# One spectral and bilinear block on one core: four edits to who computes what in the column groups

## The chip, the cores and the metric

The kernel runs on one core of a Trainium2 chip. The core has five engines with queues of their own: PE (TensorE, matmuls; PEld is its weight load), DVE (VectorE), ACT (ScalarE), POOL (GpSimd) and SP (SyncE, which here only issues DMAs). The metric is the device time of one execution in microseconds (us); lower is better. Three executions of the kernel before took 687.51, 687.57 and 688.01 us, with a median of 687.57.

## The reference

The input is one sequence x of 2048 rows and 640 columns in float32. Two residual blocks follow each other, each behind a layer normalisation without weights:

```python
h = x + irfft2(rfft2(layernorm(x)) * (w_r + 1j * w_i))
h2 = h + ((layernorm(h) @ w_gate) * (layernorm(h) @ w_up)) @ w_down
```

The first is a filter in the two-dimensional Fourier domain, the second a gated unit with 1728 hidden columns and no nonlinearity.

## The kernel before

The work runs in stages, all written for the sixteen row tiles of 128 rows.

Stage 1 (to about 39 us) loads and normalises x, folds the columns by symmetry and multiplies by a table `crs`. Its results are copied by ACT from PSUM into `s1` (`s1_copy`, L254).

The *column groups* (about 39 to 114 us) are the sixteen steps g = 0 to 15 that the change touches. For each group PE runs three pieces:

- `d_mm(g)`: the row transform, four matmuls with the table `tab` (the main part) and four with `frt` (the remainder part). It writes a PSUM pair `y`. The remainder needs `s1r`, a copy of `s1[:, 4]` split into a rounded high part and what is left, the low part. `part(g, n, engine)` makes it for n groups, for each of two halves of 64 partitions: a cast (L260) and a subtraction (L261) that reads the cast's result. Groups 0 to 2 were done on DVE, the later ones on POOL (called at the even g for groups g+5 and g+6).
- `s2_mm(g)` (L360): two matmuls on `t`, ACT's copy of the row transform (`d_out`, L353). It writes a PSUM tile, `u` or `v` (the two *twins*, one buffer each), or a pair `y` for the last two groups.
- `is2_mm(g)` (L385): the inverse products on the filtered group, into the other twin; into a pair `y` for groups 13 and 15. The first half of the pair gets the main products and the second half the remainder products.

Between the last two, DVE filters the group (`filt`, four operations): `y = v*w` (L368), the two cross products into `us` on 64 partitions each (L369, L370), and the sum `y + us` (L371). The first three read the PSUM tile and end its use; the sum has both operands in SBUF. The result `Y[g]` lies in a ring of four slots in SBUF, so group g overwrites what group g-4 left. Behind `is2_mm`, `is2_out` copies the main products into `qm` (L415, ACT) and splits the remainder products into `qr`: ACT copies them to SBUF (L420), POOL moves one row (L421), casts (L422) and subtracts (L423). For group 15 the main copy is shared by ACT (L415) and DVE (L417), and ACT and DVE split from PSUM (L427 to L431).

The order is written out in a loop over g: `s2_mm(g)`, `d_mm(g+2)`, `is2_mm(g-lag)`, `filt(g)`. `lag` begins at 0 and is raised at g = 0, 5 and 9; these three *lag steps* run no `is2_mm`, and the variable `flip` is set there: the twins change their parts, so that the next `s2_mm` writes the twin that the current filter does not read. In all other steps `s2_mm(g+1)` writes the tile that `filt(g)` reads, and waits for its L370. After the loop groups 11 to 15 are finished (L484 to L495).

Then comes the inverse row transform (to about 160 us): for each row tile `id_main` (reads `qm`, L526), `id_rest` (reads `qr`, L531), an unfolding on DVE and ACT and `is1_mm`. Its PSUM tiles are the twins in turn, with one pair `y` for tile 2. The gated unit fills the rest of the time, almost all of it PE.

Of the kernel before, what the change touches and what calls it, by code (L numbers as in the profile page):

```python
# [13 lines left out]
AF = mybir.ActivationFunctionType  # L14
OP = mybir.AluOpType

P = 128
S, D, NF, FF = 2048, 640, 321, 1728
NT = S // P
NG = 16  # L20
NQ = 322
# [27 lines left out]
def f32(ap):  # L49
    return ap.bitcast(F32)  # L50
# [11 lines left out]
def tile_spectral_glu(ctx: ExitStack, tc: tile.TileContext, x, wf, wgu, wlast, wdown, wdlast,  # L62
                      cc, ci, fmain, frem, imain, irem, mm, out):
    nc = tc.nc
# [6 lines left out]
    tt, act = nc.vector.tensor_tensor, nc.scalar.activation  # L71
# [3 lines left out]
    def banks(key, name, side="left"):  # L75
        if key in pools:
            open_pools[key].close()
        open_pools[key] = ExitStack()
        pools[key] = open_pools[key].enter_context(tc.tile_pool(name=name, bufs=2, space=bass.MemoryType.PSUM, side=side))
# [4 lines left out]
    def pair(tag):  # L84
        return pools["y"].tile([P, 2, 512], F32, tag=tag, name=tag, bufs=2)
# [4 lines left out]
    def wk(shape, name):  # L90
        return work.tile(shape, F32, tag="wk", name=name)
# [22 lines left out]
    def home(tag, shape, name, dt=F32):  # L114
        return keep.tile(shape, dt, tag=tag, name=name)

    def cut(t, o, *shape):
        v = t[:, o:o + int(np.prod(shape))]
        names = [f"d{i}" for i in range(len(shape))]
        return v.rearrange(f"p ({' '.join(names)}) -> p {' '.join(names)}", **dict(zip(names[1:], shape[1:])))  # L120
# [86 lines left out]
    def folded(t):  # L207
        o = t % NR * 1030 + 2
        return fold[:, o:o + 642], fold[:, o + 644:o + 1028]
# [44 lines left out]
            act(view(s1, 4 * t + 2048 * c, [[2048, e - c], [64, 32], [1, 4]]),  # L254
                ps[:, c * P:e * P].rearrange("p (c g m) -> p c g m", c=e - c, g=32), AF.Copy)

    def part(g, n, engine):
        for rows, k in ((slice(0, 64), 0), (slice(64, 128), 1)):
            src, hi, lo = s1[rows, 4, g:g + n], s1r[rows, k, g:g + n], s1r[64 * (1 - k):64 * (2 - k), k, g:g + n]
            engine.tensor_copy(hi, src)  # L260
            engine.tensor_tensor(lo, src, f32(hi), op=OP.subtract)  # L261

    turn = [0]

    def twin(k):
        return pools["a"].tile([P, 2, 512], F32, tag=("u", "v")[k], name=("u", "v")[k], bufs=1)
# [13 lines left out]
    for g, ts in enumerate(GROUPS):  # L280
        n = len(ts)
# [19 lines left out]
        else:  # L301
            o = crs[:, ts[0] * P:(ts[0] + n) * P].rearrange("p (t m) -> p t m", t=n)
            steps[f"t{g}"] = lambda o=o, r=r, n=n: tt(o, view(cct, 0, [[0, n], [1, P]]), view(r, 0, [[1, n], [0, P]]),
                                                      op=OP.mult)
# [6 lines left out]
    for k in order:  # L311
        if k[0] == "h":
            if k[2:] in TINY:
                done = TINY[k[2:]]
            else:
                f, j = folded(int(k[3:]))
# [3 lines left out]
            steps[k]()  # L320
    room.clear()
    banks("y", "ptwo")
    part(0, 1, nc.vector)

    WM, WI = {}, {}

# [12 lines left out]
    PD, T, PU, Y, PI = {}, {}, {}, {}, {}  # L339

    def d_mm(g):
        ps = PD[g] = pair("y")
        for c, (b, i) in enumerate(((1, 1), (1, 0), (0, 1), (0, 0))):
            mmx(ps[:, b, i * NH:(i + 1) * NH], s1[:, c, g], fmt[:, c], i == 1, False)
        for b in (1, 0):
            for l in range(2):
                mmx(ps[:, b, 0:NQ], s1r[:, 1 - b, g], frt[:, l, b], False, l == 1)

    def d_out(g):
        t = T[g] = wk([P, 2, NQ], "t")  # L350
        for c in range(2):
            for h in range(2):
                act(t[64 * c:64 * c + 64, h].rearrange("p (b f) -> p b f", b=2),  # L353
                    PD[g][64 * h:64 * h + 64, :, c * NH:(c + 1) * NH], AF.Copy)
# [6 lines left out]

    ring = [cut(home("spare", [P, 2576], "ring"), 0, 4, 2, NQ)]

    def filt(g):
        v, w = PU[g][:, :, 0:NQ], WM[g][1]
        y = Y[g] = ring[0][:, g % 4]
        us = wk([P, 2, NQ], "us")
        tt(y, v, w[:, 0], op=OP.mult)  # L368
        nc.vector.scalar_tensor_tensor(us[0:64], v[64:128], -1.0, w[64:128, 1], op0=OP.mult, op1=OP.mult)  # L369
        tt(us[64:128], v[0:64], w[0:64, 1], op=OP.mult)  # L370
        tt(y, y, us, op=OP.add)  # L371

    def is2_mm(g, k=0):
        both = pair("y") if g in (NG - 3, NG - 1) else twin(k)
        pm, pr = both[:, 0], both[:, 1]
        PI[g] = pm, pr

        def o(ps, n, c, h):
            return ps[0:n, c * 256:(c + 1) * 256].rearrange("p (a m) -> p a m", m=8)[:, :, 4 * h:4 * h + 4]

        y = Y[g]

        def one(ps, n, c, a):
            for h in range(2):
                nc.tensor.matmul(o(ps, n, c, h), y[:, h, a:a + n], inv(g, h), start=True, stop=True)  # L385

        if g == NG - 1:
            second = PI[NG - 3][0]
            PI[g] = (pm, second), pr
            one(pm, P, 0, 194)  # L390
            one(second, P, 0, 1)
            one(pr, 65, 0, 129)
            return
        one(pr, 65, 0, 129)
        one(pm, P, 0, 194)
        one(pm, P, 1, 1)

    def inv(g, h):
        return WI[g][:, h].rearrange("p (a m) -> p a m", m=4)

    def is2_out(g):
        pm, pr = PI[g]
        f = stage[g % 2]
        hi, lo = (qr[n:n + 64, :, :, 8 * g:8 * g + 8] for n in (0, 64))

        def rest(ap):
            return ap[:, 0:256].rearrange("p (r n m) -> p r n m", r=2, n=NT)

        def main(engine=None, half=None):
            o, i = qm[:, :, :, 8 * g:8 * g + 8], pm  # L410
            if half is not None:
                o, i = o[:, 2 * half:2 * half + 2], pm[half][:, 0:256]
            i = i.rearrange("p (c n m) -> p c n m", c=4 if half is None else 2, n=NT)
            if engine is None:
                act(o, i, AF.Copy)  # L415
            else:
                engine.tensor_copy(o, i)  # L417

        def split():
            act(f[0:65], pr[0:65, 0:256], AF.Copy)  # L420
            nc.gpsimd.tensor_copy(f[32:33, 128:256], f[64:65, 0:128])  # L421
            nc.gpsimd.tensor_copy(hi, rest(f[0:64]))  # L422
            nc.gpsimd.tensor_tensor(lo, rest(f[0:64]), f32(hi), op=OP.subtract)  # L423

        def split_last():
            e = f[32:33, 0:128].rearrange("p (n m) -> p n m", n=NT)
            act(hi, rest(pr[0:64]), AF.Copy)  # L427
            act(f[32:33, 0:128], pr[64:65, 0:128], AF.Copy)
            tt(lo, rest(pr[0:64]), f32(hi), op=OP.subtract)
            nc.vector.tensor_copy(hi[32:33, 1], e)  # L430
            tt(lo[32:33, 1], e, f32(hi[32:33, 1]), op=OP.subtract)  # L431

        return main, split_last if g == NG - 1 else split
# [2 lines left out]
        load_wm(g)  # L436
        load_wi(g)
    d_mm(0)
    part(1, 2, nc.vector)
    part(3, 2, nc.gpsimd)  # L440
    d_out(0)
    d_mm(1)
    d_out(1)
# [1 line left out]
    for g in range(NG - 2):  # L445
        s2_mm(g)
        d_mm(g + 2)
        if g + 3 == NG:
            xt = home("big", [P, 2, 5, 2, 512], "xt", F32R)
            irt = xt[:, 1].rearrange("p k l n -> p (k l n)")[:, 0:5 * NQ].rearrange("p (c q) -> p c q", c=5)  # L450
            nc.gpsimd.dma_start(irt, irem)
            s2_mm(NG - 2)
        if g in (0, 5, 9):
            lag += 1
            back = None
            flip = 1
        else:
            back = g - lag
            flip = 0
            is2_mm(back, 1 - turn[0])  # L460
        filt(g)
        if g % 2 == 0 and g + 5 < NG:
            part(g + 5, min(2, NG - g - 5), nc.gpsimd)
        if g + 3 < NG:
            load_wm(g + 3)
        d_out(g + 2)
        if back is not None and g + 3 < NG:
            main, split = is2_out(back)
            split()
            main()  # L470
            load_wi(back + 3)
        turn[0] ^= flip
        if g == 6:
            nc.sync.dma_start(cit, ci)
            nc.sync.dma_start(imt, imain)
            load_wi(NG - 2)
            load_wi(NG - 1)
    s2_mm(NG - 1)
    main, split = is2_out(NG - 6)
# [4 lines left out]
    for g, k in ((NG - 5, 1 - turn[0]), (NG - 4, turn[0]), (NG - 3, 0), (NG - 2, 1 - turn[0])):  # L484
        is2_mm(g, k)
        if g == NG - 5:
            filt(NG - 1)
        main, split = is2_out(g)
        split()
        main()  # L490
    is2_mm(NG - 1)
    main, split = is2_out(NG - 1)
    main(half=0)
    main(nc.vector, 1)
# [23 lines left out]
    PE_, PY, YT, Z = {}, {}, {}, {}  # L518

    def id_main(t, half=(0, 1)):  # L520
        if 0 in half:
            PE_[t] = pair("y") if t == 2 else twin((t - (t > 2) + turn[0]) % 2)
        ps = PE_[t]
        for c, (b, o) in enumerate(((0, 0), (1, 0), (0, 161), (1, 161))):
            if c // 2 in half:
                mmx(ps[:, b, o:o + 161], qm[:, c, t], imt[:, c], c < 2, False)  # L526
# [6 lines left out]
    def id_mm(t):  # L533
        id_main(t)
        id_rest(t)
# [577 lines left out]
    for n, (blk, p) in enumerate(steps):  # L1113
        if p == 6:
            s13, s12 = 2, 0
            if blk == 0:
# [27 lines left out]
                hi, lo = t34(0)  # L1144
                hi()
            else:
# [36 lines left out]
                hi, lo = t34(0)  # L1183
# [190 lines left out]
```

## Time and profile before

| what | value |
|---|---|
| median of three executions | 687.57 us |
| the profiled execution, time | 687.77 us |
| the profiled execution, span on the core | 686.0 us |
| granted TensorE clock | 0.999 |
| busy share of the span: PE, DVE, ACT, POOL | 98%, 69%, 45%, 55% |

The span runs from the first to the last instruction that the profiler recorded; the execution's own time is 1.8 us longer. All terms of the prediction are made against this one execution.

A row of the timeline reads: start in us, duration in us, engine, line, operation, output and inputs by the program's names, shapes, count, and in brackets how long the engine had been idle before, and what ended that. A row of the windows reads: the stretch in us, its length, then the busy time of PE, PEld, DVE, ACT and POOL in it with their instructions, the granted clock, and the DMA's share and rate. The matmul pieces overlap at their ends: the next one's start lies before the last one's recorded end.

### The profile page before, as it was taken

To read this page: it belongs to the slowest core of one execution; us is meant where nothing else is said; L and a number is where in the kernel's file an instruction comes from. 1 tells how busy PE (TensorE), PEld (TensorE's weight loads), DVE (VectorE), ACT (ScalarE), POOL (GpSimd) and SP (SyncE) were. 2 spreads that over 40 slices of the span, in tenths; PEclk is the share of its full clock that TensorE was granted. 3 is DMA by queue.
4 is the path that set the end of the run, shared out by engine and by line. 5 is a ranking of instruction groups with operands and counts; after the bars stand their busy time and mean duration, and the time that the engine had idled before them with its cause. 6 is when DMAs were issued, how large, how long until landed. Compare 5 with 4: busy or idle time off the path is not lost.

```text
span 686.0 us, 9960 instructions
## 1 busy us (share of the span) xinstructions
PE 674.0 (98%) x3740; PEld 593.8 (87%) x3740; DVE 471.5 (69%) x821; ACT 306.1 (45%) x568; POOL 378.9 (55%) x368
## 2 busy tenths in 40 slices
PE   8999999999999999999999999999999999999998
PEld 8888888887898988888888989888888888888987
DVE  7978887998965657576666658644757666565654
ACT  7956563488633334334334263342343333435220
POOL 2127634000296695959596534088595959778510
PEclk9999999999999999999999999999999999999999
DMA  9517771014111212121210353301212111030203
GB/s 331 199 43 227 255 245 64 1 59 147 44 59 38 78 39 77 39 77 39 77 40 28 108 208 124 130 1 39 77 38 78 39 61 55 2 114 0 77 1 153
DMA packets 23231, 60.26 MB, mean 88 GB/s; under 512 B 2576, under 2 KB 7184, under 8 KB 23184
## 3 DMA queue, kind: packets, MB, share of 16 engines
q1 hardware_dynamic: 22608, 57.92, 24.4%
q0 software_dynamic: 288, 1.48, 0.7%
q8 instruction: 29, 0.48, 0.3%
q10 hardware_dynamic: 288, 0.23, 0.1%
q14 instruction: 18, 0.15, 0.1%
HBM read 51.76 MB, written 7.86 MB: 87 GB/s over the span
## 4 chain that ended last, share of the span: by engine, by line
PE 90%; DVE 5%; DMA 3%; issue 1%; ACT 0%; POOL 0%
PE e L97 49%; PE y L97 30%; PE v L97 2%; PE u L97 2%; DMA x<-in_x_dram 2%; PE v L360 1%; PE u L385 1%; DVE us L370 1%; DVE us L369 1%; DVE ring L368 1%; PE f L229 1%; DMA bits<-in_mm_dram 1%; PE e L592 1%; PE u L360 1%; DMA cct<-in_cc_dram 1%
## 5 line engine op out<-in xcount | busy, mean ns | idle before, releaser
L97 PE MATMUL e<-xt,wst 128*128 128x512 f32 x864 | 220.4, 392 | 0.0
L97 PEld LDWEIGHTS e<-xt,wst 128*128 128x128 f32 x864 | 157.7, 188 | 26.7
L97 PE MATMUL y<-wd,ht 128*128 128x320 f32 x832 | 144.6, 311 | 0.1
L97 PEld LDWEIGHTS y<-wd,ht 128*128 128x128 f32 x832 | 131.0, 188 | 13.3 <-DVE xb L993 1.1
L782 POOL TENSOR_TENSOR wst<-raw,wst 128x1024 fp32r<-128x1024 f32 x24 | 57.8, 2409 | 130.5 <-ACT wst L781 117.7
L97 PE MATMUL e<-t,wst 128*128 128x512 f32 x288 | 75.1, 393 | 0.0
L798 POOL TENSOR_TENSOR wst<-raw,wst 128x896 fp32r<-128x896 f32 (+1 forms) x46 | 65.2, 1441 | 5.1 <-ACT wst L793 5.1
L993 DVE TENSOR_TENSOR x<-y,x 128x640 f32<-128x640 f32 x60 | 48.9, 822 | 25.6 <-PE y L97 25.2
L993 DVE TENSOR_TENSOR xb<-y,xb 128x640 f32<-128x640 f32 x60 | 49.0, 823 | 25.4 <-PE y L97 24.3
L814 ACT ACTIVATE ht<-e 128x512 fp32r<-128x512 f32 x48 | 27.5, 596 | 73.7 <-DVE rawh L911 49.7
L97 PEld LDWEIGHTS e<-t,wst 128*128 128x128 f32 x288 | 52.4, 188 | 8.8
L1081 DVE TENSOR_TENSOR m<-e,m 128x512 f32<-128x512 f32 x24 | 16.5, 687 | 50.6 <-ACT m L1074 33.4
L97 PE MATMUL y<-ex,ht 128*128 128x320 f32 x240 | 48.2, 309 | 0.0
L793 ACT ACTIVATE wst<-raw 128x896 fp32r<-128x896 f32 (+1 forms) x48 | 30.1, 677 | 34.5 <-POOL raw L787 33.7
L818 DVE TENSOR_TENSOR ht<-e,ht 128x512 fp32r<-128x512 f32 x48 | 33.1, 689 | 16.7 <-ACT ht L814 16.2
L949 ACT ACTIVATE wd<-draw 128x640 fp32r<-128x640 f32 x20 | 14.8, 741 | 65.6 <-POOL draw L962 53.9
L97 PEld LDWEIGHTS y<-ex,ht 128*128 128x128 f32 x240 | 40.2, 188 | 3.5
L97 PE MATMUL e<-xt,wdir 128*128 128x512 f32 x180 | 41.9, 391 | 0.2 <-DVE q L547 0.2
L818 POOL TENSOR_TENSOR ht<-rawh,ht 128x512 fp32r<-128x512 f32 x20 | 25.8, 1292 | 26.9 <-ACT ht L814 26.9
L97 PEld LDWEIGHTS e<-xt,wdir 128*128 128x128 f32 x180 | 33.5, 188 | 7.3 <-issue 0.6
L97 PE MATMUL e<-ht,wst 128*128 128x512 f32 x144 | 39.0, 394 | 0.0
L353 ACT ACTIVATE t<-y 64x322 f32<-64x322 f32 x64 | 27.7, 433 | 24.8 <-PE y L97 24.2
(228 smaller groups left out, 1216.4 us busy)
## 6 DMA issues: line engine op xcount, KB each, us to landing
raw<-in_wgu_dram SPq DMA_DIRECT2D x24, 640.0 KB, 3.9
wts<-in_wf_dram SPq DMA_DIRECT2D x16, 644.0 KB, 4.1
draw<-in_wdown_dram SPq DMA_DIRECT2D x24, 320.0 KB, 4.5
x<-in_x_dram SPq DMA_DIRECT2D x16, 320.5 KB, 6.0
bits<-in_mm_dram SPq DMA_DIRECT2D x32, 128.0 KB, 4.3
sp<-x SPq DMA_DIRECT2D x8, 320.0 KB, 2.2
xb<-sp SPq DMA_DIRECT2D x8, 320.0 KB, 5.5
out_dram<-x SPq DMA_DIRECT2D x8, 320.0 KB, 2.2
```

The source lines that it names most:

```text
L97: nc.tensor.matmul(o, l, r, start=start, stop=stop, skip_group_check=True)
L229: nc.tensor.matmul(PS1[t][k > 1 and t == LAST][:, k // 4, k % 4 * P:k % 4 * P + P], l, c, start=n == 0, stop=n == len(ls) - 1)
L353: act(t[64 * c:64 * c + 64, h].rearrange("p (b f) -> p b f", b=2), PD[g][64 * h:64 * h + 64, :, c * NH:(c + 1) * NH], AF.Copy)
L360: nc.tensor.matmul(ps[h][:, 0:NQ], WM[g][0][:, h], T[g][:, h], start=True, stop=True)
L782: nc.gpsimd.tensor_tensor(wa[:, 1], stage[:, 0:1024], f32(wa[:, 0]), op=OP.subtract)
L793: act(ws[:, 0, o:o + b - a], stage[:, a:b], AF.Copy)
L798: ptt(ws[:, 1, o:o + b - a], stage[:, a:b], f32(ws[:, 0, o:o + b - a]), op=OP.subtract)
L814: act(unit(u)[0], src, AF.Copy)
L818: engine.tensor_tensor(lo, src, f32(hi), op=OP.subtract)
L949: act(w[:, 0, a:b], r, AF.Copy)
L993: tt(xv, PQ[q][:, :, 0:320], xv, op=OP.add)
L1081: tt(m5, acc_a, m5, op=OP.add)
```

## The change

Four edits, all in the column groups:

1. `part` gets a fourth argument, the operation that makes the high part. For groups 0 to 2 that is now an ACT copy; the subtractions stay on DVE. For the others both stay on POOL.
2. At the three lag steps the filter's sum (`y + us`) is issued to POOL instead of DVE.
3. Group 14's filter result gets a tile of its own (from the pool `wk`) instead of a ring slot, and its split of the remainder products goes from POOL to DVE.
4. The remainder products of group 15 go to the second half of a twin instead of the second half of the pair that takes the main products. With that, the PSUM tiles of the inverse row transform are renumbered: tile 0 takes the twin `u`, tile 1 the pair `y`, and then `v` and `u` in turn.

The cut diff:

```diff
-    def part(g, n, engine):
+    def part(g, n, engine, copy):
...
-            engine.tensor_copy(hi, src)
+            copy(hi, src)
             engine.tensor_tensor(lo, src, f32(hi), op=OP.subtract)
+
+    def act_copy(o, i):
+        act(o, i, AF.Copy)
...
-    part(0, 1, nc.vector)
+    part(0, 1, nc.vector, act_copy)
...
-    def filt(g):
+    def filt(g, engine=nc.vector):
...
-        y = Y[g] = ring[0][:, g % 4]
+        y = Y[g] = ring[0][:, g % 4] if g != NG - 2 else wk([P, 2, NQ], "y")
...
-        tt(y, y, us, op=OP.add)
+        engine.tensor_tensor(y, y, us, op=OP.add)
...
-            second = PI[NG - 3][0]
+            second, pr = PI[NG - 3][0], twin(k)[:, 1]
...
-        def split():
+        def split(engine=nc.gpsimd):
...
-    part(1, 2, nc.vector)
-    part(3, 2, nc.gpsimd)
+    part(1, 2, nc.vector, act_copy)
+    part(3, 2, nc.gpsimd, nc.gpsimd.tensor_copy)
...
-        filt(g)
+        filt(g, nc.gpsimd if flip else nc.vector)
...
-        split()
+        split(nc.gpsimd if g < NG - 2 else nc.vector)
         main()
-    is2_mm(NG - 1)
+    is2_mm(NG - 1, turn[0])
...
-            PE_[t] = pair("y") if t == 2 else twin((t - (t > 2) + turn[0]) % 2)
+            PE_[t] = pair("y") if t == 1 else twin((t - (t > 1) + turn[0] + 1) % 2)
```

The lines behind `filt` stand three lower in the changed kernel: its L371 to L374 are L368 to L371 of before, L388 is L385, L423 is L420.

Three places show what moved. The first is DVE's queue at the end of stage 1, where the remainder parts of groups 0 to 2 are made, and then the first filter. Before:

```order
L246 TENSOR_TENSOR fold<-fold 128x2x160
L260 CAST s1r<-s_82 64x128
L261 TENSOR_TENSOR s1r<-s_82,s1r 64x128
L260 CAST s1r<-s_82 64x128
L261 TENSOR_TENSOR s1r<-s_82,s1r 64x128
L260 CAST s1r<-s_82 64x256
L261 TENSOR_TENSOR s1r<-s_82,s1r 64x256
L260 CAST s1r<-s_82 64x256
L261 TENSOR_TENSOR s1r<-s_82,s1r 64x256
L368 TENSOR_TENSOR ring<-u,wts 128x644
```

The same place in the changed kernel, down to the second filter:

```order
L246 TENSOR_TENSOR fold<-fold 128x2x160
L261 TENSOR_TENSOR s1r<-s_82,s1r 64x128 x2
L261 TENSOR_TENSOR s1r<-s_82,s1r 64x256 x2
L371 TENSOR_TENSOR ring<-u,wts 128x644
L372 SCALAR_TENSOR_TENSOR us<-u,wts 64x644
L373 TENSOR_TENSOR us<-u,wts 64x644
L371 TENSOR_TENSOR ring<-v,wts 128x644
```

The four casts have left DVE (they stand in ACT's queue between the last copy of stage 1 and the first `d_out`), and the second filter follows the first one's third operation.

The second place is POOL's queue from the parts of groups 3 and 4 to the first split. Before:

```order
L260 CAST s1r<-s_82 64x256
L261 TENSOR_TENSOR s1r<-s_82,s1r 64x256
L260 CAST s1r<-s_82 64x256
L261 TENSOR_TENSOR s1r<-s_82,s1r 64x256
L260 CAST s1r<-s_82 64x256
L261 TENSOR_TENSOR s1r<-s_82,s1r 64x256
L260 CAST s1r<-s_82 64x256
L261 TENSOR_TENSOR s1r<-s_82,s1r 64x256
L421 COPY bits<-bits 1x128
```

And in the changed kernel:

```order
L260 CAST s1r<-s_82 64x256
L261 TENSOR_TENSOR s1r<-s_82,s1r 64x256
L260 CAST s1r<-s_82 64x256
L261 TENSOR_TENSOR s1r<-s_82,s1r 64x256
L374 TENSOR_TENSOR ring<-ring,us 128x644
L260 CAST s1r<-s_82 64x256
L261 TENSOR_TENSOR s1r<-s_82,s1r 64x256
L260 CAST s1r<-s_82 64x256
L261 TENSOR_TENSOR s1r<-s_82,s1r 64x256
L424 COPY bits<-bits 1x128
```

The sum of group 0 stands between the parts of groups 3 and 4 and those of groups 5 and 6, which ran without a break before; the sums of groups 5 and 9 stand likewise ahead of later parts.

The third place is DVE's queue from the last filter's sum to the split of group 15. Before:

```order
L371 TENSOR_TENSOR ring<-ring,us 128x644
L417 COPY qm<-y 128x32x8
L429 TENSOR_TENSOR qr<-y,qr 64x32x8
L430 CAST qr<-bits 1x16x8
L431 TENSOR_TENSOR qr<-bits,qr 1x16x8
```

And in the changed kernel:

```order
L374 TENSOR_TENSOR ring<-ring,us 128x644
L424 COPY bits<-bits 1x128
L425 CAST qr<-bits 64x32x8
L426 TENSOR_TENSOR qr<-bits,qr 64x32x8
L420 COPY qm<-y 128x32x8
L432 TENSOR_TENSOR qr<-v,qr 64x32x8
```

Group 14's split, three operations, now stands on DVE between the last sum and DVE's half of group 15's main copy (L420 in the changed kernel).

More of the change, by code (lines that the diff above doesn't have):

```diff
@@ L417, in main @@
                 engine.tensor_copy(o, i)
-        def split():
+        def split(engine=nc.gpsimd):
             act(f[0:65], pr[0:65, 0:256], AF.Copy)
-            nc.gpsimd.tensor_copy(f[32:33, 128:256], f[64:65, 0:128])
-            nc.gpsimd.tensor_copy(hi, rest(f[0:64]))
-            nc.gpsimd.tensor_tensor(lo, rest(f[0:64]), f32(hi), op=OP.subtract)
+            engine.tensor_copy(f[32:33, 128:256], f[64:65, 0:128])
+            engine.tensor_copy(hi, rest(f[0:64]))
+            engine.tensor_tensor(lo, rest(f[0:64]), f32(hi), op=OP.subtract)
         def split_last():
@@ L460, in tile_spectral_glu @@
             is2_mm(back, 1 - turn[0])
-        filt(g)
+        filt(g, nc.gpsimd if flip else nc.vector)
         if g % 2 == 0 and g + 5 < NG:
-            part(g + 5, min(2, NG - g - 5), nc.gpsimd)
+            part(g + 5, min(2, NG - g - 5), nc.gpsimd, nc.gpsimd.tensor_copy)
         if g + 3 < NG:
```

## Prediction

> **What bounds the kernel now.** I began with the page. The profiled execution took 687.77 us around a span of 686.0; the three timed runs have a median of 687.57.
>
> ```profile
> span 686.0 us, 9960 instructions
> PE 674.0 (98%) x3740; PEld 593.8 (87%) x3740; DVE 471.5 (69%) x821; ACT 306.1 (45%) x568; POOL 378.9 (55%) x368
> ```
>
> PE is busy for 98% of the span, so nothing pays that does not shorten or close a pause of PE. The change touches only the column groups, from 38.7 to about 114 us, so next I asked which waits PE has between 36 and 115 us (columns: total, times, longest).
>
> ```profile
> PE y L97 <- DVE s1r L261: 1.5, 2, 0.8
> PE u L360 <- DVE us L370: 0.8, 1, 0.8
> PE v L360 <- DVE us L370: 0.7, 2, 0.4
> PE y L385 <- DVE ring L371: 0.6, 1, 0.6
> PE v L97 <- ACT qm L415: 0.5, 1, 0.5
> ```
>
> These are 4.1 us in all, and each line answers to one part of the change. The pauses cost more than their idle time, because matmuls overlap when they flow and restart without overlap. So I cut the stage at the starts of PE's pieces, read off the PE timeline, and compared the length of equal pieces. The first two numbers after the stretch are its length and PE's busy time.
>
> ```profile
> 38.75:41.88 3.13, 2.42 (x15) 1.75 (x14) 2.22 (x5) 0.55 (x2) 2.08 (x4) 1.00 0.00 0
> 41.88:44.60 2.72, 1.94 (x14) 1.69 (x13) 2.17 (x4) 1.73 (x4) 2.44 (x5) 1.00 0.00 0
> 45.69:47.37 1.68, 1.68 (x14) 1.68 (x13) 1.47 (x2) 0.86 (x2) 0.00 (x0) 1.00 0.21 57
> 47.37:51.93 4.56, 4.26 (x30) 3.75 (x29) 4.45 (x7) 3.29 (x8) 0.00 (x0) 1.00 0.56 168
> 51.93:56.11 4.18, 4.18 (x28) 3.84 (x29) 3.36 (x5) 2.08 (x6) 3.05 (x7) 1.00 0.71 236
> 56.11:60.21 4.10, 4.10 (x31) 3.77 (x30) 3.30 (x5) 2.66 (x7) 2.54 (x4) 1.00 0.65 227
> 67.09:72.14 5.05, 4.26 (x30) 3.76 (x29) 4.94 (x7) 3.76 (x10) 3.16 (x5) 1.00 0.66 228
> 83.19:87.88 4.69, 4.27 (x31) 3.77 (x29) 4.58 (x7) 3.42 (x8) 2.42 (x5) 1.00 0.71 235
> 105.26:106.59 1.33, 1.33 (x14) 1.33 (x13) 1.30 (x3) 0.86 (x2) 1.19 (x3) 1.00 0.90 347
> 106.59:108.66 2.07, 1.49 (x14) 1.30 (x12) 1.98 (x2) 1.32 (x4) 1.87 (x4) 1.00 0.05 12
> 108.66:110.73 2.07, 1.59 (x12) 1.35 (x12) 0.42 (x1) 0.84 (x3) 1.80 (x5) 1.00 0.00 0
> ```
>
> The row transform of one group (d_mm) takes 1.68 us when nothing stops it; those of groups 0 and 1 take 3.13 and 2.72. A full group takes 4.10; the groups behind the three lag steps take 4.56, 5.05 and 4.69, and the group behind such a pause 4.18, so 0.08 more each. One group's inverse product (is2_mm) takes 1.33; the last two pieces take 2.07 each. What could be won is therefore 1.45 + 1.04 (remainder parts), 0.54 + 1.03 + 0.67 (lag steps), 0.74 + 0.74 (end): 6.2 us.
>
> **Part 1: the high parts on ScalarE.** The handover at the start, engine by engine:
>
> ```profile
> 38.95 0.55 ACT L254 ACTIVATE s<-u 128x256 f32<-128x256 f32 x2 [0.48 <-PE u L229]
> 39.53 0.22 DVE L260 CAST s1r<-s 64x128 fp32r<-64x128 f32 x1 [2.06 <-ACT s L254]
> 39.79 0.37 DVE L261 TENSOR_TENSOR s1r<-s,s1r 64x128 fp32r<-64x128 f32 x1
> 40.09 0.72 POOL L261 TENSOR_TENSOR s1r<-s,s1r 64x256 fp32r<-64x256 f32 x1
> 40.19 0.72 DVE L260 CAST s1r<-s 64x128 fp32r<-64x128 f32 x1
> 41.48 0.56 PE L97 MATMUL y<-frt,s1r 128*128 128x322 f32 x2 [0.71 <-DVE s1r L261]
> 42.14 1.78 ACT L353 ACTIVATE t<-y 64x322 f32<-64x322 f32 x4 [2.63 <-PE y L97]
> 42.27 0.55 DVE L261 TENSOR_TENSOR s1r<-s,s1r 64x256 fp32r<-64x256 f32 x1
> ```
>
> The same cast takes 0.22 us on DVE alone and 0.72 beside GpSimd's subtraction. Now four ACT copies replace the four DVE casts. ACT idled 2.63 us there. The nearest row for an ACT copy of this size (busy us, then mean ns of one):
>
> ```profile
> L427 ACT ACTIVATE qr<-y 64x256 fp32r<-64x256 f32 x1 | 0.4, 365 | 0.0
> ```
>
> At 0.37 us apiece for 256 columns, and less for 128, all four are done by 41.0 (39.5, where ACT's last copy of the stage before ends, and four times 0.37). DVE's first subtraction then runs from about 39.9 to 40.3; the second ends at 40.8 if it follows at once (0.37 to 0.55 by the rows of DVE's L261), or at 41.4 if GpSimd's 0.72 subtraction goes in between. Before, PE got it at 41.48. So the first transform wins between 0.1 and 0.7 us. The third and fourth subtraction, 0.55 each, end by 41.9, or by 43.2 if GpSimd goes in between once more (41.4 + 0.55 + 0.72 + 0.55). The second transform starts 0.1 to 0.7 us before 41.88 and needs the fourth for its last two matmuls, at the earliest 1.68 - 0.56 = 1.12 us on: 42.3 to 42.9. Its 1.04 goes whole, or all but 0.3. d_out(0), the ACT piece at 42.14 behind 2.63 us of idling, can follow PE at once, since ACT is through with its copies by then. Sum 0.85 to 1.75; I take 1.4, somewhat above the middle, because a loss at both transforms needs GpSimd to go first twice.
>
> The Trainium skill ("SBUF — State Buffer", Who interferes with whom) says that a DVE instruction with two SBUF inputs and a GpSimd instruction that reads SBUF exclude each other for a whole instruction; by that rule GpSimd would get in between each time that it started first, and this term would be nearer to 0.85.
>
> **Part 2: three sums on GpSimd.** At a lag step two filters follow each other on DVE with only 2.77 us of PE work between their inputs (4.10 without the 1.33 of is2_mm), and the fourth operation of the first holds up the second. The four operations:
>
> ```profile
> L371 DVE TENSOR_TENSOR ring<-ring,us x16: 828/830/1323, 48.4 to 107.4; 128x644 f32<-128x644 f32 x16
> 47.57 0.82 DVE L370 TENSOR_TENSOR us<-u,wts 64x644 f32<-64x644 f32 x1
> 50.14 1.49 PE L385 MATMUL u<-bits,ring 128*65 128x128 f32 x12
> L953 POOL TENSOR_TENSOR wd<-draw,wd 128x640 fp32r<-128x640 f32 x20 | 31.1, 1576 | 0.0
> ```
>
> Without the sum, 0.83 to 1.32 us, DVE can begin the next filter as soon as its input is there. In a flowing group the chain of input, three operations and release fits: PE has no wait there but those listed. How near it is, the group that starts at 51.93 tells: its first operation starts at 53.29 (a row further down), three operations at 0.83 end 2.5 us later, 3.85 after the group's start, and 4.10 are to be had. So all three pauses should go, by a margin of 0.25 less the release of PE. GpSimd's price for 128x644 I take from the 128x640 row: 1.58. Its sums for groups 5 and 9 are used two to three groups later, over 6 us: hidden. That of group 0 is not: shifted by part 1's gain (1.4) with everything else, L370 ends at 47.0, GpSimd starts 0.1 later and ends at 48.7; is2_mm(0) wants it at 48.7, its weight load 0.15 before. So 0.2 to 0.25 of the 0.54 comes back as a new wait: term 0.3, range 0 to 0.54. The other two: 1.03 and 0.67. Queued behind each sum on GpSimd are remainder parts and splits; they slip behind the sum's end, at group 0 to 48.7 us, but the parts so delayed are for group 5, whose transform PE runs in iteration 3, two to three groups of 4.1 us later. That covers it; without that cover each us of slip would be a us of wait.
>
> **Part 3: the end of the groups.** The rows:
>
> ```profile
> 101.55 0.83 DVE L368 TENSOR_TENSOR ring<-y,wts 128x644 f32<-128x644 f32 x1 [0.72 <-PE u L385]
> 107.38 1.23 DVE L371 TENSOR_TENSOR ring<-ring,us 128x644 f32<-128x644 f32 x1
> 108.20 0.38 ACT L420 ACTIVATE bits<-u 65x256 f32<-65x256 f32 x1 [0.47 <-PE u L385]
> 109.93 0.42 DVE L417 COPY qm<-y 128x256 f32<-128x256 f32 x1 [1.32 <-PE y L385]
> 110.30 0.38 ACT L415 ACTIVATE qm<-y 128x256 f32<-128x256 f32 x1 [1.23 <-PE y L385]
> ```
>
> The filter of group 14 waited 0.72 us for is2_mm(10), whose ring slot it overwrites; with a tile of its own it doesn't. Then the last sum starts at about 106.6 and ends at 107.4 (at 0.83) to 107.9 (at 1.3), all on the clock of before. PE can begin group 15 at 106.59 + 1.33 = 107.92. The 0.74 goes, or 0.5 of it: I take 0.67.
>
> The other 0.74 stands before id_main(0), which waited for ACT's copy at 110.30, and that waited for the remainder products that shared its tile. In the other bank pair they no longer hold it: with PE's start at 107.92 the copy ends near 109.4. But DVE's copy of the other half (L417) now stands behind group 14's split, three new DVE operations that cannot start before ACT's copy at 108.20 has ended (108.58): about 0.22 + 0.22 to 0.72 + 0.37 to 0.55 us, by the DVE casts and subtractions of part 1, that is until 109.4 to 110.1, and later by another 0.72 if GpSimd's subtraction for group 13 gets in between. L417 ends 0.42 later, between 109.8 and 111.2. id_main(0) wants it half way through its piece, about 0.6 after its start (an estimate: half of a piece a little shorter than is2_mm's 1.33), at 107.92 + 1.33 + 0.6 = 109.85. So 0 to 1.3 us of new waiting stands against 0.74: term 0.05, range -0.5 to 0.74.
>
> **Behind the groups.**
>
> ```profile
> 110.70:152.00 41.30, 41.27 (x255) 36.98 (x256) 38.09 (x108) 22.70 (x49) 1.32 (x4) 1.00 0.05 21
> DVE q L546 <- ACT s L542: 2.0, 1, 2.0
> ```
>
> In the next stage PE and DVE (third busy time) are both close to full. DVE's run starts after a 2.0 us wait for ACT, which waits for PE, so it moves along with PE, and the gain is kept to the end.
>
> **Sum.** 1.4 + 0.3 + 1.03 + 0.67 + 0.67 + 0.05 = 4.1 us. 687.77 - 4.1 = 683.65 for a profiled execution, which stood 0.2 above the median: 683.45. With all lower ends (0.85, 0, 0.95, 0.59, 0.5, -0.5; the lag steps without what the next group loses) 2.4 us, 685.2; with all upper ends (1.75, 0.54, 1.03, 0.67, 0.74, 0.74) 5.5 us, 682.1.
>
> **Rivals.** *The end gives its share back and GpSimd gets between all subtractions and comes late with its first sum*: lower ends throughout, 685.2. For it: casts three times as long beside GpSimd. Against: it needs all of them. Chance 0.13.
>
> *DVE keeps the gain.* DVE is nearly as full as PE in the stage behind (38.09 of 41.30 us); if its run starts when it did, nothing arrives: 687.6. Against: the wait at its head, which PE sets. Chance 0.06.
>
> *GpSimd's sum shuts out DVE* (the slower side). If DVE's three filter operations of the next group stand still while a sum of length h runs, each lag step loses h against the flowing case: 687.57 - 2.1 (parts 1 and 3) - 2.24 + 3h. At 1.58 that is 688.0, within 0.2%; it turns slower from h = 1.9; stretched by 0.5 as the cast was (0.72 against 0.22), h is 2.08 and the time 689.5.
>
> ```profile
> 53.29 0.83 DVE L368 TENSOR_TENSOR ring<-v,wts 128x644 f32<-128x644 f32 x1 [0.76 <-PE v L360]
> 53.45 0.73 POOL L423 TENSOR_TENSOR qr<-bits,qr 64x256 fp32r<-64x256 f32 x1
> ```
>
> For it: L371's 1.32 and the 0.72 cast. Against: these two rows, a filter operation with an operand in PSUM at its usual 0.83 beside a GpSimd subtraction at its usual 0.73; only L371, with both operands in SBUF, is ever stretched, and that is the one that leaves. Chance 0.06: 0.05 slower, 0.01 the same.
>
> **How the numbers follow.** The forecast has 0.75, the first rival 0.13; both are faster. About 0.2%, 1.4 us, is what a measurement tells here from no change. Faster 0.88, same 0.07, slower 0.05. The range runs from 682.2 to 685.3, which holds the forecast's ends and the first rival.
>
> **What would show it.** Right: no PE wait for s1r of over 0.4 us; groups behind the lag steps at 4.1 to 4.2; L368-L370 (now L371 to L373) still 0.83 beside the sums; a wait of 0.1 to 0.3 at is2_mm(0); id_main(0) waiting for DVE instead of ACT. Wrong: filter operations stretched beside a GpSimd sum, waits of PE between 111 and 152 us that were not there, or a sum much over 1.6 us.

## The result and the profile after

The changed kernel took 683.68 us (median of four executions, 683.30 to 683.78), the kernel before 687.54 beside it: the ratio is 0.9942, with a 95% interval from 0.9925 to 0.9959. That is 3.86 us faster, where 4.1 were forecast. Times here are medians; of all executions behind them one, of the kernel with the sums alone, was slow (834.03 us at a granted clock of 0.753), and it moves that kernel's median from 685.06 to 685.13. The profiled execution took 683.78 us around this span:

```profile
span 682.0 us, 9958 instructions
PE 673.3 (99%) x3740; PEld 593.9 (87%) x3740; DVE 469.0 (69%) x817; ACT 307.7 (45%) x572; POOL 382.3 (56%) x368
```

The waits of PE in the changed kernel between 30 and 165 us:

```profile
PE u L97 <- DVE qm L420: 0.7, 1, 0.7
PE e L97 <- DVE q L550: 0.2, 1, 0.2
PE y L97 <- DVE s1r L261: 0.2, 1, 0.2
```

Of the five lines of before, four are gone or nearly so: the lag steps (L370, now L373) and the last sum (L371, now L374) appear no more, and s1r is down from 1.5 to 0.2. The fifth has changed its releaser: PE now waits 0.7 us for DVE's copy, not for ACT's. The same cut of PE's pieces as in the prediction, in the changed kernel (stretch, length, PE busy first):

```profile
38.94:41.56 2.62, 2.41 (x15) 1.74 (x14) 1.43 (x3) 2.00 (x6) 1.58 (x4) 1.00 0.00 0
41.56:43.25 1.69, 1.69 (x15) 1.69 (x13) 0.97 (x2) 1.45 (x4) 0.72 (x1) 1.00 0.00 0
46.03:50.22 4.19, 4.19 (x31) 3.72 (x30) 3.85 (x6) 2.94 (x7) 2.86 (x4) 1.00 0.53 153
50.22:54.32 4.10, 4.10 (x30) 3.76 (x29) 3.21 (x5) 2.43 (x7) 3.67 (x7) 1.00 0.81 268
65.31:69.40 4.09, 4.09 (x30) 3.76 (x29) 3.74 (x6) 2.84 (x7) 3.20 (x5) 1.00 0.68 230
69.40:73.53 4.13, 4.13 (x30) 3.79 (x29) 3.31 (x5) 2.53 (x7) 2.95 (x5) 1.00 0.91 281
80.42:84.52 4.10, 4.10 (x31) 3.76 (x29) 3.76 (x6) 2.85 (x7) 3.13 (x6) 1.00 0.70 227
84.52:88.65 4.13, 4.13 (x31) 3.79 (x30) 3.31 (x5) 2.53 (x7) 2.26 (x4) 1.00 0.80 267
103.18:104.51 1.33, 1.33 (x14) 1.33 (x13) 1.05 (x2) 0.86 (x2) 1.24 (x2) 1.00 0.07 20
104.51:106.07 1.56, 1.50 (x14) 1.25 (x12) 0.74 (x2) 1.16 (x4) 1.35 (x4) 1.00 0.00 0
106.07:108.21 2.14, 1.47 (x8) 1.23 (x9) 2.00 (x5) 0.62 (x2) 1.00 (x3) 1.00 0.00 0
```

Three pieces of before are needed beside those that the prediction shows, the groups behind the pauses at groups 5 and 9 and id_main(0):

```profile
72.14:76.32 4.18, 4.18 (x28) 3.85 (x29) 3.36 (x5) 1.62 (x5) 1.65 (x3) 1.00 0.82 252
87.88:92.06 4.18, 4.18 (x28) 3.84 (x29) 3.37 (x5) 1.96 (x6) 1.40 (x3) 1.00 0.67 226
110.73:111.94 1.21, 1.21 (x9) 1.21 (x10) 0.64 (x2) 0.48 (x2) 1.00 (x3) 1.00 0.00 0
```

Set against the same pieces of before, each term of the sum can be read off (in us):

| term | before | after | won | forecast |
|---|---|---|---|---|
| transforms of groups 0 and 1 | 3.13 + 2.72 | 2.62 + 1.69 | 1.54 | 1.4 |
| lag step at group 0 | 4.56 + 4.18 | 4.19 + 4.10 | 0.45 | 0.3 |
| lag step at group 5 | 5.05 + 4.18 | 4.09 + 4.13 | 1.01 | 1.03 |
| lag step at group 9 | 4.69 + 4.18 | 4.10 + 4.13 | 0.64 | 0.67 |
| up to group 15's products | 2.07 | 1.33 | 0.74 | 0.67 |
| those products and id_main(0) | 2.07 + 1.21 | 1.56 + 2.14 | -0.42 | 0.05 |

The sum is 3.96 us. The last line is the one that came out other than taken: the end gives back 0.42 us. The rows of the changed kernel there:

```profile
105.30 0.43 DVE L424 COPY bits<-bits 1x128 f32<-1x128 f32 x1 [1.03 <-ACT bits L423]
105.73 0.72 POOL L426 TENSOR_TENSOR qr<-bits,qr 64x256 fp32r<-64x256 f32 x1
105.76 0.83 DVE L425 CAST qr<-bits 64x256 fp32r<-64x256 f32 x1
106.63 0.42 DVE L426 TENSOR_TENSOR qr<-bits,qr 64x256 fp32r<-64x256 f32 x1
107.08 0.42 DVE L420 COPY qm<-y 128x256 f32<-128x256 f32 x1
107.56 0.82 PE L97 MATMUL u<-tab,qm 128*128 128x161 f32 x4 [0.67 <-DVE qm L420]
```

Group 14's split waits for ACT's copy, then takes 1.7 us on DVE, with a cast of 0.83 us beside GpSimd's subtraction for group 13, and only then comes the copy for which PE stands still.

### The profile page after: what moved, and what is told of

The parts are those of the page before. It is cut to its first block, busy times and chain, and to the rows that moved or that the text cites. A ratio compares the mean times of both kernels' runs of the same rounds, so it can differ in the third digit from the quotient of the medians.

```text
span 682.0 us, 9958 instructions
## 1 busy us (share of the span) xinstructions
PE 673.3 (99%) x3740; PEld 593.9 (87%) x3740; DVE 469.0 (69%) x817; ACT 307.7 (45%) x572; POOL 382.3 (56%) x368
## 4 chain that ended last, share of the span: by engine, by line
PE 93%; DMA 3%; DVE 2%; POOL 1%; ACT 0%; issue 0%; ACTq 0%
PE e L97 50%; PE y L97 32%; PE v L97 2%; PE u L97 2%; PE u L388 2%; DMA x<-in_x_dram 2%; PE v L363 1%; PE f L229 1%; PE u L363 1%; DMA bits<-in_mm_dram 1%; PE e L595 1%; DMA cct<-in_cc_dram 1%; PE u L229 1%; PE v L388 1%; PE v L229 0%; PE y L363 0%
## 5 line engine op out<-in xcount | busy, mean ns | idle before, releaser
L509 POOL TENSOR_TENSOR wd<-draw,wd 128x640 fp32r<-128x640 f32 x8 | 15.1, 1910 | 40.8 <-ACT wd L508 40.8
```

The lines of the kernel that those rows point to most:

```text
L509: los.append(lambda r=r, a=a, b=b: engine.tensor_tensor(w[:, 1, a:b], r, f32(w[:, 0, a:b]), op=OP.subtract))
```

## Experiments

The theory: each wait of PE in the groups was closed as forecast, and what is missing was lost to the place of group 14's split on DVE. The rivals: DVE in the stage behind keeps part of the gain, the GpSimd sums cost DVE something, or the parts of the change don't add up.

**The end of the groups.** Four kernels on one chip. The yardstick first, which is the changed kernel without an edit.

> The changed kernel once more, as the yardstick for its neighbours in this call. Theory (each wait of PE closed, 0.4 us lost again before id_main(0) because group 14's split stands ahead of DVE's half of the copy): 683.7, within 0.3. Rival (DVE keeps part of the gain in the inverse row transform, and the size varies with it): differs from 683.68 by more than 0.5.

It took 683.91 us against 687.76 of before (ratio 0.9942, 0.9929 to 0.9954).

The second keeps the split on GpSimd:

```diff
-        split(nc.gpsimd if g < NG - 2 else nc.vector)
+        split()
```

> As changed, but group 14's split stays on GpSimd. Theory: DVE's half of group 15's copy (L420) starts as soon as its products are there, about 105.7 instead of 107.08 on the trace's clock, the 0.67 us wait of PE before the second half of id_main(0) goes, and GpSimd's split ends near 108.1, when id_rest(0) wants it: 0.8 to 1.1 us faster than the changed kernel, 682.6 to 682.9. Rival (the split had to leave GpSimd, since it comes too late for id_rest(0) there): PE waits there instead, within 0.3 of 683.7 or slower.

Measured: 682.73 us, 1.18 faster than the yardstick (ratio to before 0.9926, 0.9912 to 0.9940), and 0.95 faster than the 683.68 of the first measurement. The rows of this kernel:

```profile
105.44 0.42 DVE L420 COPY qm<-y 128x256 f32<-128x256 f32 x1 [1.40 <-PE y L388]
107.11 0.72 POOL L426 TENSOR_TENSOR qr<-bits,qr 64x256 fp32r<-64x256 f32 x1
107.27 0.71 DVE L434 TENSOR_TENSOR qr<-bits,qr 1x128 fp32r<-1x128 f32 x1
108.04 0.99 PE L97 MATMUL u<-xt,qr 128*128 128x322 f32 x5
```

DVE's copy now waits for PE and not for the split, and both splits are through (107.83 and 107.98) just before id_rest(0) starts at 108.04, without a wait. The rival, that GpSimd is too late with it, falls. In this trace group 15's products and id_main(0) take 2.78 us (104.27 to 107.05), where the changed kernel took 3.70 and the kernel before 3.28. The -0.42 of the table is therefore 0.50 won less 0.92 lost to the split's place.

The third keeps the split on DVE, but behind the copy:

```diff
-        split(nc.gpsimd if g < NG - 2 else nc.vector)
+        split(rest_=g < NG - 2)
+        split14 = split
...
     main(nc.vector, 1)
+    split14(nc.vector, copy=False)
     split()
```

(`split` is cut in two there: ACT's copy stays in its place, the other three operations are issued by the second call.)

> As changed, but DVE does its half of group 15's copy first and group 14's split behind it. Theory: no wait in id_main(0), but DVE's three split operations now stand ahead of group 15's split, whose last operation ends near 108.8 while id_rest(0) wants it near 108.3: 0.3 to 0.7 us faster than the changed kernel, 683.0 to 683.4. Rival (the wait in id_main(0) is not due to the order on DVE): no change, 683.7.

Measured: 682.67 us, 1.24 faster than the yardstick, more than expected. In its rows the cast runs in 0.29, since GpSimd has finished, and group 15's split ends at 107.90, in the moment in which id_rest(0) wants it:

```profile
105.30 0.42 DVE L420 COPY qm<-y 128x256 f32<-128x256 f32 x1 [1.40 <-PE y L388]
106.20 0.29 DVE L428 CAST qr<-bits 64x256 fp32r<-64x256 f32 x1
107.62 0.28 DVE L437 TENSOR_TENSOR qr<-bits,qr 1x128 fp32r<-1x128 f32 x1
107.90 0.99 PE L97 MATMUL u<-xt,qr 128*128 128x322 f32 x5
```

The loss is thus shown to be the order on DVE: the same three operations on the same engine cost about 1 us ahead of the copy (1.24 by the medians, 0.93 by the pieces in the traces), and no wait of PE behind it. My 0.3 to 0.7 had priced the cast as if GpSimd still worked beside it.

The fourth takes the own tile away:

```diff
-        y = Y[g] = ring[0][:, g % 4] if g != NG - 2 else wk([P, 2, NQ], "y")
+        y = Y[g] = ring[0][:, g % 4]
```

> As changed, but group 14's filter result goes to its ring slot again, so that the filter waits for is2_mm(10), 0.7 us. Theory: the last sum ends 0.7 later, PE waits about 0.5 before group 15's products, but DVE's copy is held by the split of group 14 until 107.1 in any case, so nothing arrives: within 0.2 of the changed kernel, 683.7. Rival (each wait closed counts by itself, as the prediction summed it, 0.67 for this one): 684.3.

Measured: 683.63 us (683.47 to 683.92, the yardstick 683.45 to 684.05): no difference. The wait is back in the list of this kernel's waits, and yet DVE's copy stands where it stood (106.72 in the yardstick):

```profile
PE y L388 <- DVE ring L374: 0.6, 1, 0.6
PE y L97 <- DVE s1r L261: 0.2, 1, 0.2
```

```profile
106.78 0.42 DVE L420 COPY qm<-y 128x256 f32<-128x256 f32 x1
107.92 1.26 PE L97 MATMUL y<-tab,qm 128*128 128x161 f32 x8
```

So one part of the change, the tile of its own for group 14, was worth nothing as long as the split stood ahead of the copy. The next kernel does the same with the split on GpSimd (both edits above together):

> As changed, but group 14's split on GpSimd and its filter result in the ring slot. Theory (the own tile's gain was hidden behind the split on DVE, and shows once the split is away): the 0.6 us wait of PE before group 15's products is now paid in full, 0.5 to 0.75 slower than the run with the split on GpSimd alone (682.73): 683.2 to 683.5. Rival (the own tile is worth nothing at all): 682.7.

Measured: 683.32 us against the 682.73 with the tile, 0.59 slower. The two were timed on different chips, but the kernel before took nearly the same on both (687.73 and 687.76 us), the ranges are apart (683.08 to 683.64 and 682.66 to 682.78), and the traces agree: from the first transform to id_main(1) it takes 68.85 us without the tile and 68.32 with it. There the tile pays.

**The parts alone.** Each is the kernel before with one part of the change's diff.

> The kernel before with edit 1 alone (high parts of groups 0 to 2 by ScalarE). Theory: the time between the first transform's start and s2_mm(0) falls from 5.85 to 4.3 us as in the changed kernel's trace, and all of it arrives: 1.5 us faster than before, 686.1. Rival (part of it is given back at the first lag step, where DVE holds up PE all the same): 0.5 to 1.0 faster, 686.8.

Measured: 686.16 us against 687.79, 1.63 faster (ratio 0.9976, 0.9967 to 0.9985), as expected; the three waits at the lag steps are all still there.

> The kernel before with edit 2 alone (three sums on GpSimd). Theory: 0.45 + 1.01 + 0.64 = 2.1 us faster than before, 685.5. Rival (GpSimd's sum shuts out DVE's next filter): not faster, 687.6 or more.

Measured: 685.13 us, 2.66 faster (ratio 0.9960, 0.9947 to 0.9973): more than the 2.1.

> The kernel before with edits 3 and 4 alone (own tile, split of group 14 on DVE, remainder products in the other bank pair). Theory: 0.74 won at group 15 and 0.4 lost before id_main(0): 0.2 to 0.5 us faster than before, 687.2. Rival (both waits of 0.74 gone, as if the split on DVE were free): 1.5 faster, 686.1.

Measured: 687.38 us, 0.41 faster (ratio 0.9995, 0.9986 to 1.0003), not clear of no change, as expected.

Alone the parts win 1.63 + 2.66 + 0.41 = 4.70 us, together 3.86. The traces show where 0.67 of the 0.84 us between them comes from. From the start of PE's last piece of stage 1 to s2_mm(0) the kernel before takes 6.65 us (37.95 to 44.60), part 1 alone 5.12, the sums alone 5.98, the whole 5.12. The sums alone win 0.67 there, which part 1 wins too and which the whole can have only once. The rows on DVE of the kernel with the sums alone say why:

```profile
41.43 0.78 DVE L260 CAST s1r<-s 64x256 fp32r<-64x256 f32 x1
42.24 0.42 DVE L261 TENSOR_TENSOR s1r<-s,s1r 64x256 fp32r<-64x256 f32 x1
42.69 0.29 DVE L260 CAST s1r<-s 64x256 fp32r<-64x256 f32 x1
43.02 0.42 DVE L261 TENSOR_TENSOR s1r<-s,s1r 64x256 fp32r<-64x256 f32 x1
47.86 1.57 POOL L371 TENSOR_TENSOR ring<-ring,us 128x644 f32<-128x644 f32 x1 [5.80 <-DVE us L370]
```

GpSimd now waits for the filter at the head of its queue, 5.80 us, and so leaves DVE alone: the last cast takes 0.29 us. In the kernel before, GpSimd went on with its next parts, and the same cast took 0.72:

```profile
42.61 0.80 POOL L261 TENSOR_TENSOR s1r<-s,s1r 64x256 fp32r<-64x256 f32 x1
42.85 0.72 DVE L260 CAST s1r<-s 64x256 fp32r<-64x256 f32 x1
```

The other 0.17 us is left open.

**Contention at the start.** The whole change with GpSimd held back for its first parts, by a copy of one column that reads DVE's last result:

```diff
+    nc.gpsimd.tensor_copy(small.tile([P, 1], F32, tag="hold", name="hold"), f32(s1r[:, 1, 2, P - 1:P]))
     part(3, 2, nc.gpsimd, nc.gpsimd.tensor_copy)
```

> As changed, but GpSimd begins the parts of groups 3 and 4 only when DVE has finished group 2's (a one-column copy on GpSimd that reads DVE's last result stands ahead of them). Theory (DVE's subtractions with two operands in SBUF wait for whole GpSimd instructions): DVE's four subtractions take about 0.3 to 0.42 each instead of 2.50 us together, the 0.20 wait of PE in d_mm(0) goes: 0.2 to 0.4 us faster than the changed kernel. Rival (the subtractions are paced by ACT's copies): no change in PE's wait and within 0.1 of the changed kernel, 683.7.

Measured: 683.14 us, 0.54 under the changed kernel's 683.68 (ratio to before 0.9933, 0.9922 to 0.9945). The changed kernel was not timed beside it; against the kernel before beside it (687.79) the gain is 4.65 us, where the changed kernel had 3.86, so the size of the step is 0.4 to 0.8. The subtractions between 38 and 46 us (minimum, median and maximum in ns), first in the changed kernel, then here:

```profile
L261 DVE TENSOR_TENSOR s1r<-s,s1r x4: 285/636/839, 40.1 to 41.7; 64x128 fp32r<-64x128 f32 x2, 64x256 fp32r<-64x256 f32 x2
```

```profile
L261 DVE TENSOR_TENSOR s1r<-s,s1r x4: 286/354/421, 39.8 to 41.0; 64x128 fp32r<-64x128 f32 x2, 64x256 fp32r<-64x256 f32 x2
```

GpSimd's presence had nearly doubled their median, 636 against 354 ns. The wait for s1r is gone from PE's list, and the way from stage 1 to s2_mm(0) falls from 5.12 to 4.69 us, so 0.43 of the gain is seen in the trace. The rival, that ACT's copies set the pace of the changed kernel, falls. With GpSimd held they come next: DVE waits 0.15 us for ACT before the third subtraction.

**More sums on GpSimd.** The suspected cost in every iteration of the loop:

```diff
-        filt(g, nc.gpsimd if flip else nc.vector)
+        filt(g, nc.gpsimd)
```

(The last two groups' sums, outside that loop, stay on DVE: fourteen on GpSimd, where the expectation says sixteen.)

> As changed, but every filter's sum on GpSimd (16 instead of 3). Theory: DVE's other three operations keep 0.83 us beside them, since one of their operands is in PSUM; what can grow late is GpSimd's own queue, which gets 1.6 us per group on top of about 1.3 for parts and 1.5 for splits, 4.4 in 4.1: PE waits for results or splits, 684 to 688. Rival (a sum on GpSimd shuts out DVE's filter): DVE's operations stretched to 1.5 us and more, over 690.

Measured: 684.70 us (ratio 0.9957, 0.9942 to 0.9972). The operations of this kernel's filter:

```profile
L372 DVE SCALAR_TENSOR_TENSOR us<-v,wts x9: 829/830/831, 48.0 to 95.4; 64x644 f32<-64x644 f32 x9
```

```profile
L374 POOL TENSOR_TENSOR ring<-ring,us x14: 1542/1558/1568, 47.0 to 98.3; 128x644 f32<-128x644 f32 x14
```

With a GpSimd sum in every iteration no operation of DVE that reads PSUM grows by a hundredth. What grows is GpSimd's queue: between 44 and 96 us GpSimd is busy for 45.0 us, against 35.0 in the changed kernel, and one of DVE's filters now waits 1.7 us for a sum. Two waits of PE are new, 0.4 us for a sum and 0.2 for a DMA, and the kernel is 0.8 to 1.0 us slower than the change (683.91 and 683.68). That GpSimd's fuller queue is what costs this is argued from these waits; no run tests it alone.

**The best of it.** Both gains together, in either form:

> As changed, with group 14's split on GpSimd and GpSimd's parts of groups 3 and 4 held until DVE is through. Theory: the two gains add, since one lies before the first s2_mm and the other behind the last: 682.73 less 0.5 is 682.2. Rival: one eats the other, 682.7.

Measured: 682.45 us (ratio 0.9922, 0.9910 to 0.9935).

> As changed, with DVE's copy ahead of group 14's split and GpSimd's parts of groups 3 and 4 held until DVE is through. Theory: as for the neighbour, 682.67 less 0.5 is 682.2. Rival: 682.7.

Measured: 682.24 us (ratio 0.9921, 0.9908 to 0.9935), 5.5 us under the kernel before. Against the same kernels without the hold, timed on another chip (682.73 and 682.67), that is 0.28 and 0.43: the gains add, if somewhat short of the 0.5. PE has one wait left between 30 and 160 us in it, and that lies behind the groups:

```profile
PE e L97 <- DVE q L556: 0.2, 1, 0.2
```

## Why the prediction was right

*The bound* was read rightly: PE, by its pauses, and each pause by its lost length rather than its idle time. The listed waits were 4.1 us, the pieces said 6.2, and 3.96 were won with 0.7 still visible as a wait. That the total came so close to the 4.1 is partly luck: the first five terms won 4.38 where 4.07 was taken, and the last came out 0.47 under its forecast. (The range begins at 682.2, though its own upper ends add up to 682.1.)

*Part 1* won 1.54 where 1.4 was taken from 0.85 to 1.75. The four ACT copies took 1.52 us in its trace, 0.38 apiece, as priced. GpSimd did get between the subtractions (up to 839 ns), but only the first transform noticed, with a wait of 0.2 us. The prices for the subtractions, 0.37 to 0.55, were all from rows beside GpSimd; with GpSimd held they take 0.29 and 0.42. Nor was the cast of 0.22 alone, as I read it: GpSimd's own cast ran beside it, from 39.57 us, but had started 0.04 later. The exclusion that the Trainium skill states ("SBUF — State Buffer", Who interferes with whom) agrees with the stretched subtractions and with their return to 421 ns at most once GpSimd is held; the 0.85 that I tied to it was too low, since the fourth subtraction ended at 42.56 and the second transform ran through without a wait.

*Part 2*: the sums took 1.56 to 1.57 us against 1.58 from the nearest row. The second filter kept its pace beside the first sum:

```profile
47.22 1.56 POOL L374 TENSOR_TENSOR ring<-ring,us 128x644 f32<-128x644 f32 x1 [4.94 <-DVE us L373]
47.31 0.83 DVE L371 TENSOR_TENSOR ring<-v,wts 128x644 f32<-128x644 f32 x1 [0.27 <-PE v L363]
48.15 0.83 DVE L372 SCALAR_TENSOR_TENSOR us<-v,wts 64x644 f32<-64x644 f32 x1
49.00 0.82 DVE L373 TENSOR_TENSOR us<-v,wts 64x644 f32<-64x644 f32 x1
```

The loss forecast at is2_mm(0), 0.2 to 0.25, is 0.09 (4.19 against 4.10), too short to be listed as a wait: the sum ends at 48.78, and PE starts at 48.83.

*Part 3*: the mechanism was named, DVE's copy behind group 14's split; the size was off. The step set 0 to 1.3 us of new waiting against 0.74 and took 0.05 for the rest. It was -0.42, near the lower end of the range. With the split out of the way the end won 0.50 and not 0.74, as PE's weight load for id_main(0) still waits 0.3 us for ACT's half of the copy; and the split ahead of DVE's half cost 0.92 where about 0.69 was taken. Two of its operations were priced too low: the copy of one row took 0.43 us and the cast 0.83, both beside a GpSimd operation that had started just before, where I had 0.22 and 0.22 to 0.72. And I counted the tile of its own as 0.67 beside it; the experiments show that this and the split's cost are not two terms but one chain, of which only the later end counts. That the trace shows the 0.74 as won and the 0.42 as lost does not contradict this: without the tile the first is not won and the second not lost.

*The rivals.* DVE in the stage behind kept nothing: from the start of id_main(1) to the first product of the gated unit it took 46.71 us before (111.94 to 158.65) and 46.70 after (108.21 to 154.91). The sum that shuts out DVE is refuted by the rows above, three times and fourteen times over. Of the first rival, the share given back at the end came true. GpSimd did get between subtractions, at the price of one wait of 0.2 us, and its first sum was late by 0.09; the term of 0.85 and the full loss at group 0 did not come.

## What to carry to other kernels

Measure a pause by comparing whole pieces of the same work, since a restart costs more than the idle gap: at group 5 a listed wait of 0.8 us lengthened the work by 1.03. When an operation moves to another engine, look at what it stands ahead of in the new queue: here three short operations cost about 1 us ahead of one copy, and nothing behind it. Two waits on one chain are not two gains, and a part tested alone may win what another part wins too.

## What the runs showed of the hardware

DVE's instructions with all operands in SBUF stretch beside GpSimd work: a 64x256 cast from 0.29 to 0.83 us, a subtraction on a single partition from 0.28 to 0.71. Those with an operand in PSUM kept their 0.83 us beside every sum on GpSimd. A wait at the head of GpSimd's queue can therefore speed DVE up: in the kernel with the sums alone it won 0.67 us at a place that the edit doesn't touch.

GpSimd is stretched by DVE in the same way. In the changed kernel its cast took 0.95 us, where it takes 0.39 elsewhere, behind a sum on DVE:

```profile
49.85 0.83 DVE L374 TENSOR_TENSOR ring<-ring,us 128x644 f32<-128x644 f32 x1
49.98 0.95 POOL L260 CAST s1r<-s 64x256 fp32r<-64x256 f32 x1
```

These rows bear on whether the stretch is a whole instruction's exclusion or a finer sharing. In three of the pairs shown, the instruction that started first keeps its usual time (the sum here its 0.83, GpSimd's subtractions of 105.73 in the changed kernel and of 107.11 in the second experiment their 0.72), and the other ends 0.14 to 0.25 us after it. A sharing would have stretched both, so the rows speak for an exclusion.
